# A long convolution beside an MLP on one core: the two octet transforms as one block, on three fixed two-bank PSUM tiles that the MLP's first product shares

## The chip, the cores and the metric

The kernel runs on one core of a Trainium2 chip. The metric is device microseconds (us) of one launch. Before the change the median of three runs is 364.56 us (364.38 to 364.85).

A core has a matrix engine (TensorE; PE in the profile, its weight loads PEld), a vector engine (VectorE; DVE), a scalar engine (ScalarE; ACT), GpSimd (POOL) and SyncE (SP). They run side by side and wait for each other through semaphores. Matrix products land in PSUM, which this kernel allocates in eight banks of 512 float32 numbers per partition; everything else is computed from SBUF. SP, ACT and POOL each issue transfers between DRAM and SBUF. Each engine works through its own list of instructions in order: an instruction that waits holds up all that stand behind it on that engine.

## The reference, cut to what matters

```
# S = 2048 rows, D = 448 channels, F = 1792, all float32
xn  = layernorm(q)
ks  = shift conv of k with 4 taps           # per channel
kv  = ks * v
y   = causal convolution of kv with ssm_k (length 2048, by FFT of 4096) + ssm_D * kv
out = q + xn * y + (mish(xn @ w1 + b1) @ w2)
```

There are two branches, a gated long convolution and a two-layer MLP, and their sum with q is the output.

## The kernel before, in words

**The MLP** sets the beat. The rows are taken in 8 chunks of 256, and F in 7 pieces of 256, which makes 56 pairs (chunk, piece), and two *slots* for each pair. Each float32 operand of a product is split in a high and a low part, and three products are added. In the even slot 2i stands `g1_mm(i)` (L499): 22 matmuls of 256 columns into one PSUM bank, the hidden layer transposed. In the odd slot 2i+1 stand `mish(i)` and `g2_mm(i-2)`. `mish` is, on ACT, two activations (L507) that read that bank and a cast to the high part `ach` (L79), and on DVE the low part `acl` (L80). `g2_mm` is 12 matmuls of 448 columns (L528 to L530) into two further banks, where the output of a chunk is summed.

For the first five chunks the normalised rows are transposed on PE: `ln_T` (L452) writes four small transposes into a bank of the same pool as `g1_mm`'s, ACT casts it to `XH` (L464), and DVE subtracts to `XL` (L462). That happens twice for a chunk, each time for 128 of its rows: T0 behind the `g1_mm` of the last pair but one of the chunk ahead, T1 just before the `g1_mm` of its last pair. Chunk 0 is transposed at the start in other banks.

**The convolution** is an FFT written as float32 matmuls in small tiles, put into the slots by hand: `at(slot, ...)` puts a piece ahead of the MLP's instructions of that slot, `after(slot, ...)` behind them. It has three stages.

- *F1* (slots up to 59): blocks of 8 small matmuls (L130; the profile shows each small float32 matmul as two, x16) on the filter `h` and on `kv`; ACT copies one half (L136), DVE folds (L140), and the results go to DRAM as `Dh` and `Dkv`.
- *The octets* (slots 63 to 90): eight parts. For octet o a block H transforms the filter (`ah`, read from `Dh`) and a block V the signal (`av`, read from `Dkv`). Both are `f2_mm` (L219), 16 small matmuls of 448 columns each (x32 in the profile), in two halves, real and imaginary. ACT copies both results to SBUF as `hs` (L230) and `vs` (L239). DVE multiplies them (`prod`, L252 for its arithmetic). A block I1 (L262), of 16 more, goes back; ACT copies its result to `qe` (L270) and issues two stores of it to `E` in DRAM (L273). V stands at slot s = 65, 68, ..., 86, H one slot earlier (63 for the first), I1 at s + 4. The last I1 stands at slot 90.
- *I2* (slots 98, 102, 106, 110): POOL loads `e` from `E` (L295), DVE folds (L301, L303), a block of 8 small matmuls for each of two chunks (L319) finishes the convolution, and DVE gates it and adds it to the rest.

**PSUM before:** `g1p`, two tiles of one bank, for `g1_mm`, the transposes and the fillers at the start; `g2p`, two of one bank; `pcp`, two tiles `pc` of two banks, that all of F1, F2, I1 and I2 take in turn. A tile is handed out anew for each use, and a use waits until the tile's last reader is done.

**At the start** `g1_mm(0)` writes both banks of `g1p`, its two column blocks in turn, and each of the first two activations reads one of them; ACT casts weights (L354) between these two.

## Time and profile before

| what | value |
|---|---|
| median of three runs | 364.56 us (364.38 to 364.85) |
| the profiled execution, its own time | 364.74 us |
| its span, from first to last instruction | 363.0 us |
| mean granted TensorE clock | 0.999 |
| busy: DVE, ACT, POOL | 74%, 46%, 20% of the span |
| g1 matmuls (XH by w1h, one of the groups) | 448 of 285 ns, 90.6 us |
| F2 matmuls on ah; on av | 256 of 542 ns; 256 of 543 ns |
| stores of E, from issue to landing | 5.8 us each |

The span is the time from the first to the last instruction; 1.7 us of the execution's time lie around it. In a row of the timeline the first number is the start, the second the length; matmuls overlap, so that a row's length is more than its share of the engine. `[0.62 <-ACT XH L464]` at a row's end says that the engine stood idle for 0.62 us before it and what ended that. `<-` in a row puts the output before the inputs. A view of windows gives, for each stretch, its length, then PE, PEld, DVE, ACT and POOL busy with instruction counts, then the granted clock, the DMA share and GB/s. In a row of the groups stand, after the count, the busy time and the mean ns of one, then the idle time before and its releaser.

### The profile page before, as it was taken

How to read it: one execution, taken by the hardware profiler on the slowest of the kernel's cores; microseconds unless marked ns; L12 is line 12 of the kernel's file. 1: busy time of each engine (PE TensorE's matmuls, PEld its weight loads, DVE VectorE, ACT ScalarE, POOL GpSimd, SP SyncE). 2: the span in 40 equal slices, each digit the busy share in tenths (PEclk: the TensorE clock that was granted, in tenths of full speed). 3: DMA queues.
4: the chain of work that ended last, by engine and by line, in shares of the span. 5: the costliest groups of instructions: out<-in, count | busy, mean ns of one | idle time of the engine just before them, and what ended most of it. 6: DMA issues, size and time to landing. Idle time of an engine off the chain costs nothing.

```text
span 363.0 us, 7466 instructions
## 1 busy us (share of the span) xinstructions
PE 357.0 (98%) x3108; PEld 290.0 (80%) x3108; DVE 268.0 (74%) x367; ACT 166.6 (46%) x279; POOL 71.4 (20%) x66
## 2 busy tenths in 40 slices
PE   8999999999999999999999999999999999999995
PEld 2988888888888988988977666666666889889885
DVE  5999658999998988797427755767665744997641
ACT  4966553343424323334254555647655534225450
POOL 2136003722037224513000020000010005112020
PEclk9999999999999999999999999999999999999999
DMA  7998969758686438615877798998897486969655
GB/s 247 363 369 307 414 248 275 182 175 270 156 260 199 105 101 255 152 60 144 226 245 231 252 257 210 289 258 218 284 283 172 93 251 216 404 246 279 105 71 132
DMA packets 32451, 81.69 MB, mean 225 GB/s; under 512 B 2977, under 2 KB 18978, under 8 KB 32418
## 3 DMA queue, kind: packets, MB, share of 16 engines
q1 hardware_dynamic: 21266, 47.16, 39.3%
q10 hardware_dynamic: 8240, 19.38, 21.8%
q0 software_dynamic: 2912, 14.69, 13.5%
q8 instruction: 24, 0.39, 0.5%
q14 instruction: 9, 0.07, 0.1%
HBM read 52.77 MB, written 28.45 MB: 224 GB/s over the span
## 4 chain that ended last, share of the span: by engine, by line
PE 49%; DMA 4%; DVE 2%; ACT 1%; ACTq 1%; issue 0%
PE pg L499 18%; PE pg L528 7%; PE pc L219 6%; PE pg L530 6%; PE pg L529 6%; PE pc L262 4%; PE pc L319 2%; DMA av<-Dkv 2%; DMA Dkv<-st 2%; ACTq L273 1%; DVE st L140 1%; DVE x L183 1%; ACT a L507 0%; DVE qt L535 0%; DVE x L186 0%
## 5 line engine op out<-in xcount | busy, mean ns | idle before, releaser
L507 ACT ACTIVATE a<-pg,b1t 128x256 f32<-128x256 f32 x112 | 47.2, 473 | 108.7 <-PE pg L499 95.4
L499 PE MATMUL pg<-XH,w1h 128*128 128x256 f32 x448 | 90.6, 285 | 0.2 <-DVE XL L462 0.2
L499 PEld LDWEIGHTS pg<-XH,w1h 128*128 128x128 f32 x448 | 69.6, 188 | 18.6 <-issue 16.5
L528 PE MATMUL pg<-w2h,ach 128*128 128x448 f32 x224 | 83.2, 371 | 0.0
L530 PE MATMUL pg<-w2h,acl 128*128 128x448 f32 x224 | 81.4, 363 | 0.0
L80 DVE TENSOR_TENSOR acl<-a,ach 128x512 fp32r<-128x512 f32 x56 | 39.1, 698 | 57.1 <-ACT ach L79 57.0
L529 PE MATMUL pg<-w2l,ach 128*128 128x448 f32 x224 | 81.2, 362 | 0.0
L499 PE MATMUL pg<-XL,w1h 128*128 128x256 f32 x448 | 71.3, 277 | 0.0
L499 PEld LDWEIGHTS pg<-XL,w1h 128*128 128x128 f32 x448 | 60.2, 188 | 0.0
L499 PE MATMUL pg<-XH,w1l 128*128 128x256 f32 x336 | 56.8, 278 | 0.0
L528 PEld LDWEIGHTS pg<-w2h,ach 128*128 128x128 f32 x224 | 42.0, 187 | 14.4 <-issue 11.5
L499 PEld LDWEIGHTS pg<-XH,w1l 128*128 128x128 f32 x336 | 46.8, 188 | 0.0
L530 PEld LDWEIGHTS pg<-w2h,acl 128*128 128x128 f32 x224 | 42.1, 188 | 2.6
L529 PEld LDWEIGHTS pg<-w2l,ach 128*128 128x128 f32 x224 | 42.1, 188 | 2.4
L140 DVE TENSOR_TENSOR st<-pc,st 128x896 f32<-128x896 f32 x32 | 34.8, 1089 | 4.5 <-ACT st L136 3.8
L79 ACT CAST ach<-a 128x512 fp32r<-128x512 f32 x56 | 34.7, 620 | 1.8
L166 POOL TENSOR_TENSOR x<-kr,skb 128x896 f32<-128x896 f32 x8 | 17.0, 2130 | 78.2 <-DVE x L165 56.8
L183 DVE TENSOR_TENSOR x<-x 128x896 f32<-128x896 f32 x24 | 26.4, 1098 | 2.8 <-POOL x L166 2.2
L403 POOL TENSOR_TENSOR mv<-ve,mhalf 128x2 f32<-128x2 f32 x3 | 3.8, 1251 | 98.1 <-DVE ve L400 98.1
L136 ACT COPY st<-pc 128x896 f32<-128x896 f32 x16 | 14.5, 907 | 14.2 <-PE pc L130 12.6
L407 POOL TENSOR_SCALAR xn<-qt,mv,rstd 128x448 f32<-128x448 f32 x8 | 20.5, 2566 | 0.4
L270 ACT COPY qe<-pc 128x896 f32<-128x896 f32 x16 | 13.8, 912 | 12.0 <-PE pc L262 12.0
(83 smaller groups left out, 384.4 us busy)
## 6 DMA issues: line engine op xcount, KB each, us to landing
Dkv<-st ACTq DMA_DIRECT2D x16, 448.0 KB, 6.3
ah<-Dh SPq DMA_DIRECT2D x8, 896.0 KB, 7.9
av<-Dkv SPq DMA_DIRECT2D x8, 896.0 KB, 6.9
E<-qe ACTq DMA_DIRECT2D x16, 448.0 KB, 5.8
e<-E POOLq DMA_DIRECT2D x8, 896.0 KB, 8.4
kr<-in_k_dram SPq DMA_DIRECT2D x10, 448.0 KB, 6.4
Dh<-st ACTq DMA_DIRECT2D x10, 448.0 KB, 5.9
x<-in_hT_dram SPq DMA_DIRECT2D x8, 448.0 KB, 6.5
```

Of the source, the lines that this page charges most:

```text
L79: nc.scalar.copy(h, raw)
L80: V.tensor_sub(l, raw, h)
L140: f(st[:, n], e, st[:, 1])
L166: nc.gpsimd.tensor_mul(o, KR[g - u // 2], skb[:, u:u + 1].to_broadcast([128, 2, D]))
L183: V.tensor_add(KV[g], KV[g], o)
L219: nc.tensor.matmul(p[32 * t:32 * t + 32, r, :D], g[rs, t, c], a[rs, t], start=True, stop=True, tile_position=(64 * r, 32 * t))
L407: eng.tensor_scalar(xn[:, jj, :D], Q[c][:, jj], mv[:, j, 0:1], rs(c)[:, jj:jj + 1], op0=ALU.subtract, op1=ALU.mult)
L499: nc.tensor.matmul(ps[n], l, r, start=all(m[0] != n for m in seq[:n_]), stop=all(m[0] != n for m in seq[n_ + 1:]))
L507: nc.scalar.activation(a[:, n], ps[n], AF.Mish, bias=b1t[:, 2 * p + n:2 * p + n + 1])
L528: nc.tensor.matmul(ps, ah[:, n, cs], w2h[:, f], start=f == 0, stop=False)
L529: nc.tensor.matmul(ps, ah[:, n, cs], w2l[:, f], start=False, stop=False)
L530: nc.tensor.matmul(ps, al[:, n, cs], w2h[:, f], start=False, stop=f == NF - 1)
```

## The change

It does five things.

1. **PSUM.** The pools `g1p` and `pcp` are gone. In their place stand three tiles of two banks that are made once, `pp`, `pq` and `pr` (`duo`). `pg()` hands out the two banks of `pp` in turn to `g1_mm`, the transposes and the fillers. F1 takes `pq` and `pr`, I2 too.
2. **The octets.** H and V of an octet are one block `hv_mm` at slot s = 66, 69, ..., 87: H in two tiles, then V in two, of which one is a tile that H has just used, behind its copy by ACT. For even s the order of the tiles is pp, pq, pr, pp; for odd s pr, pq, pp, pr. I1 of octet o-1 stands at s + 2, and the last at slot 90: I1 of octet 6 at slot 89. A table `GB` gives the first products in these slots banks of `pr` and `pp`.
3. **The product.** DVE reads V in PSUM, in its four multiplications; `vs` and the 16 copies to it are gone. Subtraction and addition follow. In odd slots `mish` stands ahead of the block, and its split (ACT and DVE) behind the four multiplications (`held`).
4. **The stores** of `E` are issued by POOL instead of ACT.
5. **Buffers.** `hs` has one buffer instead of two, `av`, `ya` and `yc` two instead of one. `ah` and `av` of an octet are both loaded three slots ahead (the first at 59 and 63).

```diff
-    g1p = pool("ps_g1", 2, space=PSUM)
     g2p = pool("ps_g2", 2, space=PSUM)
-    pcp = pool("ps_c", 2, space=PSUM)
+    psp = pool("ps", space=PSUM)
+    duo = [psp.tile([128, 2, 512], F32, name=n) for n in ("pp", "pq", "pr")]
...
+    def bank(n):
+        return duo[n // 2][:, n % 2]
...
+    def pg():
+        turn[0] += 1
+        return bank(turn[0] % 2)
...
-        PS[key, g] = ps = [pc(), pc()]
+        PS[key, g] = ps = [pc(1), pc(2)]
...
+    def hv_mm(o, hb, vb):
+        PS["H", o] = [f2_mm(AH[o], o, c, hb[c]) for c in range(2)]
+        h_out(o)
+        PS["V", o] = [f2_mm(AV[o], o, c, vb[c]) for c in range(2)]
+        AH.pop(o), AV.pop(o)
...
-            nc.scalar.copy(PV[o][:, c], p[:, :, :D])
...
+    def prod(o):
+        vr, vi = (p[:, :, :D] for p in PS.pop(("V", o)))
+        hs = HS.pop(o)
...
+        for x, *y in ((a, vr, hr), (c, vr, hi), (b, vi, hi), (e, vi, hr)):
+            V.tensor_mul(x, *y)
+        for fn in held:
+            fn()
...
-            nc.scalar.dma_start(E.rearrange("p (k h) d -> p k h d", h=2)[:, k:k + 4, o // 4], qe[64 * r:64 * r + 64])
+            nc.gpsimd.dma_start(E.rearrange("p (k h) d -> p k h d", h=2)[:, k:k + 4, o // 4], qe[64 * r:64 * r + 64])
...
-        pt = [g1p.tile([128, 2, CH], F32, name="pg1") for _ in range(2 if i == 0 else 1)]
+        pt = [(bank(GB[i]) if i in GB else pg()).rearrange("p (a b) -> p a b", a=2) for _ in range(2 if i == 0 else 1)]
...
+        hb, vb, ib = ((0, 1), (2, 0), (2, 1)) if s % 2 == 0 else ((2, 1), (0, 2), (0, 2))
...
+        at(s, hv_mm, o, hb, vb)
...
+            at(s + 2, i1_mm, o - 1, ib)
...
+    at(s + 3, i1_mm, o, (0, 1))
+    after(s + 3, i1_out, o)
```

The order of the instructions shows what this makes of three places. A row is an instruction with its line, its output and inputs, the shape of one, how many stand in a row, and in brackets the engines (or queues) whose semaphores it waits for. Line numbers are those of each kernel's own source (g1 is L499 before and L504 after, the transposes L452 and L456, F2 L219 and L227, the `qe` copies L270 and L274). The sign `_49` belongs to the semaphores' names.

First PE at the end of chunk 0, where the second transposition T1 of chunk 1 is followed by the pair's first product. Before:

```order
L130 MATMUL pc<-x,idr 64x448 [waits DMAHW1_49,DVE_49,PE_49]
L130 MATMUL pc<-x,idr 64x448 x7
L452 MATMUL pg_544<-idr,xn 128x128 [waits Activation_49,Pool_49]
L452 MATMUL pg_544<-idr,xn 128x128 x2
L452 MATMUL pg_544<-idr,xn 128x128 [waits Pool_49]
L499 MATMUL pg_551<-XH,w1h 128x256 [waits DVE_49]
L499 MATMUL pg_551<-XH,w1h 128x256 x2
```

After:

```order
L138 MATMUL pq<-x,idr 64x448 x2
L138 MATMUL pr<-x,idr 64x448 x2
L456 MATMUL pp<-idr,xn 128x128 [waits DVE_49,Activation_49,Pool_49]
L456 MATMUL pp<-idr,xn 128x128 x2
L456 MATMUL pp<-idr,xn 128x128 [waits Pool_49]
L504 MATMUL pp<-XH,w1h 128x256 [waits DVE_49]
L504 MATMUL pp<-XH,w1h 128x256 x2
```

The rows keep their places; the tile is now one, `pp`, for both. Before, the DVE semaphore's value at L499 was that of the subtraction `XL` of T0, whose bank the product takes over; in the program after, it is that of `XL` of T1, which reads the transposes that stand just ahead. So it is at each of the four chunk changes with transposes. Elsewhere `g1_mm(i+1)` waits in the program after for the second activation of `mish(i)`, where it waited for that of `mish(i-1)`, or of none, before; and at the start the first activation waits for all of `g1_mm(0)`, where it waited for its own bank's part.

Then PE in the octets. Before, a V block behind the odd slot's `g2_mm` (H stands in the same form one slot earlier):

```order
L528 MATMUL pg_2085<-w2h,ach 128x448
L529 MATMUL pg_2085<-w2l,ach 128x448
L530 MATMUL pg_2085<-w2h,acl 128x448
L219 MATMUL pc<-av,g 32x448 [waits DMAHW1_49,Activation_49]
L219 MATMUL pc<-av,g 32x448 x7
L219 MATMUL pc<-av,g 32x448 [waits Activation_49]
L219 MATMUL pc<-av,g 32x448 x7
L499 MATMUL pg_2344<-XH,w1h 128x256 x3
```

After, the block of an odd slot:

```order
L227 MATMUL pr<-ah,g 32x448 [waits DMAHW2_49,DMAHW1_49]
L227 MATMUL pr<-ah,g 32x448 x7
L227 MATMUL pq<-ah,g 32x448 [waits Activation_49]
L227 MATMUL pq<-ah,g 32x448 x7
L227 MATMUL pp<-av,g 32x448 [waits DMAHW3_49,Activation_49]
L227 MATMUL pp<-av,g 32x448 x7
L227 MATMUL pr<-av,g 32x448 [waits Activation_49]
L227 MATMUL pr<-av,g 32x448 x7
L536 MATMUL pg_2008<-w2h,ach 128x448
```

H and V stand in one piece, and V's last half waits for ACT, which copies H out of the same tile.

Last ACT at the end of the octets, the copies and stores of octets 6 and 7. Before:

```order
L270 COPY qe<-pc 128x896 [waits DMAHW7_49,DMAHW6_49,PE_49]
L270 COPY qe<-pc 128x896 [waits PE_49]
L273 DMA E<-qe 64x4x448 [waits DMAHW0_49,Activation_49]
L273 DMA E<-qe 64x4x448 [waits DMAHW2_49]
L507 ACTIVATE a<-pg_3333,b1t 128x256 [waits PE_49]
L507 ACTIVATE a<-pg_3333,b1t 128x256
L79 CAST ach<-a 128x512 [waits Activation_49]
L270 COPY qe<-pc 128x896 [waits DMAHW2_49,DMAHW0_49,PE_49]
L270 COPY qe<-pc 128x896 [waits PE_49]
L273 DMA E<-qe 64x4x448 [waits DMAHW3_49,Activation_49]
L273 DMA E<-qe 64x4x448 [waits DMAHW4_49]
```

After:

```order
L274 COPY qe<-pp 128x896 [waits DMASW3_49,DMASW4_49,DVE_49,PE_49]
L274 COPY qe<-pr 128x896 [waits DVE_49,PE_49]
L274 COPY qe<-pp 128x896 [waits DMASW5_49,DMASW6_49,PE_49,Activation_49]
L274 COPY qe<-pq 128x896 [waits PE_49]
L512 ACTIVATE a<-pr,b1t 128x256 [waits DVE_49,PE_49]
L512 ACTIVATE a<-pr,b1t 128x256
```

The stores have left ACT's list, and the copies of octet 7 now follow directly on those of octet 6. `qe` has one buffer before and after: the copies of octet 7 wait for the two stores of octet 6 (DMASW5 and DMASW6), which used to lie three slots back and now lie one.

More of the change, by code (lines that the diff above doesn't have):

```diff
@@ L28 @@
 POOL_H = {20: (0, 2)}
-H0_AT = 63
-OCT_AT = (65, 3)
+OCT_AT = (66, 3)
 I2_AT = {98: (6, 7), 102: (0, 1), 106: (2, 3), 110: (4, 5)}
@@ L80, in split, with pc @@
         V.tensor_sub(l, raw, h)
-    def pc():
-        return pcp.tile([128, 2, 512], F32, name="pc")
+    def pc(n):
+        return duo[n]
+    def bank(n):
+        return duo[n // 2][:, n % 2]
+    turn = [0]
+    def pg():
+        turn[0] += 1
+        return bank(turn[0] % 2)
     drip = []
@@ L191, in tile_kernel @@
     sp2 = []
-    GT, AH, AV, HS, PV, Y = {}, {}, {}, {}, {}, {}
+    GT, AH, AV, HS, Y = {}, {}, {}, {}, {}
     def t2(shape, name, bufs=1):
@@ L204, in o_load @@
             GT[o] = [g]
-        d[o] = t2([128, 4, D], name)
+        d[o] = t2([128, 4, D], name, 2 if d is AV else 1)
         nc.sync.dma_start(d[o], src[16 * o:16 * o + 16].rearrange("(t a) n d -> (a n) t d", t=4))
@@ L211, in gi_load, with f2_mm @@
         GT[o].append(gi)
-    def f2_mm(a, o, c):
-        p = pc()
+    def f2_mm(a, o, c, n):
+        p = pc(n)
         g = GT[o][0]
@@ L221, in f2_mm, with h_out, i1_mm @@
         return p
-    def h2_mm(o):
-        PS["H", o] = [f2_mm(AH[o], o, c) for c in range(2)]
-        AH.pop(o)
-    def h2_out(o):
-        HS[o] = t2([128, 2, 2, D], "hs", 2)
+    def hv_mm(o, hb, vb):
[3 more added lines that the diff above has]
+        AH.pop(o), AV.pop(o)
+    def h_out(o):
+        HS[o] = t2([128, 2, 2, D], "hs")
         for c, p in enumerate(PS.pop(("H", o))):
             nc.scalar.copy(HS[o][:, c], p[:, :, :D])
-    def v2_mm(o):
-        PS["V", o] = [f2_mm(AV[o], o, c) for c in range(2)]
-        AV.pop(o)
-    def v2_out(o):
-        PV[o] = t2([128, 2, 2, D], "vs")
-        for c, p in enumerate(PS.pop(("V", o))):
-            nc.scalar.copy(PV[o][:, c], p[:, :, :D])
-    def prod(o, part):
-        vs, hs = PV[o], HS[o]
-        vr, vi, hr, hi = vs[:, 0], vs[:, 1], hs[:, 0], hs[:, 1]
-        if part == 0:
-            Y[o] = a, c, b, e = [t2([128, 2, D], n) for n in ("ya", "yc", "yb", "yd")]
-            ops = ((V.tensor_mul, a, vr, hr), (V.tensor_mul, b, vi, hi), (V.tensor_sub, a, a, b))
-        else:
-            a, c, b, e = Y[o]
-            ops = ((V.tensor_mul, c, vr, hi), (V.tensor_mul, e, vi, hr), (V.tensor_add, c, c, e))
-            del PV[o], HS[o]
-        for f, *x in ops:
-            f(*x)
-            dv()
-    def i1_mm(o):
+    def prod(o):
+        vr, vi = (p[:, :, :D] for p in PS.pop(("V", o)))
+        hs = HS.pop(o)
+        hr, hi = hs[:, 0], hs[:, 1]
+        a, c = Y[o] = [t2([128, 2, D], n, 2) for n in ("ya", "yc")]
+        b, e = [t2([128, 2, D], n) for n in ("yb", "yd")]
+        for x, *y in ((a, vr, hr), (c, vr, hi), (b, vi, hi), (e, vi, hr)):
+            V.tensor_mul(x, *y)
+        for fn in held:
+            fn()
+        held.clear()
+        dv(2)
+        V.tensor_sub(a, a, b)
+        dv()
+        V.tensor_add(c, c, e)
+        dv()
+    def i1_mm(o, ib):
         gi = GT[o][1]
-        ps = [pc(), pc()]
+        ps = [pc(n) for n in ib]
         for c in range(2):
@@ L312, in i2_mm @@
     def i2_mm(c):
-        p = pc()
+        p = pc(1 + c % 2)
         e = EE.pop(c)
@@ L469, in ln_T @@
             x_tiles(c)
-        p = g1p.tile([128, 2, CH], F32, name="pg1").rearrange("p a b -> p (a b)")
+        p = pg()
         transposes(c, jj, p)
@@ L473, in ln_T @@
             x_split(c, jj, p, lo)
-    AHL, P1, P2 = {}, {}, {}
+    AHL, P1, P2, GB = {}, {}, {}, {}
+    held, hv = [], set()
     pairs = [(c, p) for c in range(NCHUNK) for p in range(NP)]
@@ L513, in mish @@
         al = mp.tile([128, 2, CH], F32R, name="acl", bufs=3)
-        split(ah, al, a)
-        dv()
         AHL[i] = ah, al
+        if 2 * i + 1 in hv:
+            held.append(lambda: split(ah, al, a))
+        else:
+            split(ah, al, a)
+            dv()
     def g2_mm(i, jjs=(0, 1)):
@@ L564, in mlp_slot @@
                     ln_T(c + 1, 0)
-                mish(i)
+                if s not in hv:
+                    mish(i)
             if 0 <= j < n - 1:
@@ L612, in tile_kernel @@
         s, d = OCT_AT[0] + OCT_AT[1] * o, OCT_AT[1]
-        h = s - 1 if o else H0_AT
-        (at if o else after)(h - d if o else h - 4, o_load, AH, Dh, o, "ah")
-        at(s - d if o else s - 2, o_load, AV, Dkv, o, "av")
-        at(h, h2_mm, o)
-        after(h, h2_out, o)
-        at(s, v2_mm, o)
-        after(s, v2_out, o)
-        at(s, gi_load, o)
-        after(s + 1, prod, o, 0)
-        after(s + 2, prod, o, 1)
-        at(s + 4, i1_mm, o)
-        after(s + 4, i1_out, o)
+        hb, vb, ib = ((0, 1), (2, 0), (2, 1)) if s % 2 == 0 else ((2, 1), (0, 2), (0, 2))
+        (at if o else after)(s - d if o else s - 7, o_load, AH, Dh, o, "ah")
+        at(s - d if o else s - 3, o_load, AV, Dkv, o, "av")
+        at(s, hv_mm, o, hb, vb)
+        at(s, gi_load, o)
+        after(s, prod, o)
+        if s % 2:
+            hv.add(s)
+        if o:
+            at(s + 2, i1_mm, o - 1, ib)
+            after(s + 2, i1_out, o - 1)
+        if s % 2 == 0:
+            GB[s // 2], GB[s // 2 + 1] = 2, 0
+        else:
+            GB[s // 2 + 1] = 2
+    at(s + 3, i1_mm, o, (0, 1))
+    after(s + 3, i1_out, o)
+    GB[(s + 3) // 2] = 4
     ts = sorted(I2_AT)
@@ L682, in tile_kernel @@
     x_tiles(0)
-    fill = g1p.tile([128, 2, CH], F32, name="pg1").rearrange("p a b -> p (a b)")
+    fill = pg()
     def filler(n, w=wz):
@@ L714, in tile_kernel @@
             g2_evac(pairs[j][0])
+        if s in hv:
+            mish(s // 2)
         for fn, args in plan.pop(s, ()):
@@ L719, in tile_kernel @@
         for fn, args in fns:
-            if fn in (h2_out, v2_out, i1_out):
+            if fn is i1_out:
                 fn(*args)
         for fn, args in fns:
-            if fn not in (h2_out, v2_out, i1_out):
+            if fn is not i1_out:
                 fn(*args)
```

## The prediction

> **What bounds the kernel.** I read the span and the engines' shares first, then the windows (length, then PE, PEld, DVE, ACT, POOL busy, clock, DMA share, GB/s), one for the F1 stage and one for the octets.

> ```profile
> span 363.0 us, 7466 instructions
> PE 357.0 (98%) x3108; PEld 290.0 (80%) x3108; DVE 268.0 (74%) x367; ACT 166.6 (46%) x279; POOL 71.4 (20%) x66
> 20.00:160.00 140.00, 139.79 (x1087) 123.39 (x1080) 123.68 (x171) 58.83 (x104) 46.22 (x31) 1.00 0.71 224
> 185.00:290.00 105.00, 104.50 (x1143) 72.64 (x1142) 68.02 (x83) 57.87 (x87) 3.69 (x4) 1.00 0.82 234
> ```

> PE has no idle time to give: 0.21 us in 140, 0.50 in 105. So a saving counts only if PE spends less time on its own instructions, and any new wait of PE is added to the end in full, because nothing later has slack to take it back. DVE is near full only up to 160 us (123.68 of 140). The question is thus what PE now has to wait for. The order shows it: `g1_mm`, the transposes and `mish` share one tile, `pp`, and a product waits for the last reader of the whole tile, where it used to wait for the reader of its own bank.

> **Start: +2.6.**

> ```profile
> 10.95 0.48 ACT L507 ACTIVATE a<-pg,b1t 128x256 f32<-128x256 f32 x1
> 11.31 1.05 ACT L354 CAST w1h<-kr 128x1024 fp32r<-128x1024 f32 x1
> 12.25 0.48 ACT L507 ACTIVATE a<-pg,b1t 128x256 f32<-128x256 f32 x1
> 14.51 0.84 ACT L507 ACTIVATE a<-pg,b1t 128x256 f32<-128x256 f32 x2 [0.28 <-PE pg L499]
> 11.48 0.62 PE L499 MATMUL pg<-XH,w1h 128*128 128x256 f32 x3
> 14.31 0.50 PE L499 MATMUL pg<-XH,w1h 128*128 128x256 f32 x3
> ```

> The first product's second pair starts at 11.48, so pair 0 ends just ahead. Now the first activation waits for all of pair 0 (11.49 instead of 10.95, +0.54), and pair 1 for the second activation. Between them stands the cast, 12.25 − 10.95 = 1.30 from activation to activation: 11.49 + 1.30 + 0.48 = 13.27, then PE at 13.3, +1.8. Pair 1 takes 14.31 − 11.48 less its present waits, about 2.67, to 15.97; pair 2 now waits for the 0.84 of `mish(1)`: 16.9 instead of 14.31, +2.6. Before, pair 2 waited for `mish(0)` alone.

> **Four chunk changes: +10.7.** First the product behind T1, then the subtraction that ends `XL` of the same T1, for chunks 1 to 4.

> ```profile
> 38.21 0.60 PE L499 MATMUL pg<-XH,w1h 128*128 128x256 f32 x3
> 78.00 0.60 PE L499 MATMUL pg<-XH,w1h 128*128 128x256 f32 x3
> 117.97 0.60 PE L499 MATMUL pg<-XH,w1h 128*128 128x256 f32 x3
> 155.97 0.62 PE L499 MATMUL pg<-XH,w1h 128*128 128x256 f32 x3 [0.20 <-DVE XL L462]
> 39.11 0.69 DVE L462 TENSOR_TENSOR XL<-pg,XH 128x512 fp32r<-128x512 f32 x1 [0.62 <-ACT XH L464]
> 80.92 0.68 DVE L462 TENSOR_TENSOR XL<-pg,XH 128x512 fp32r<-128x512 f32 x1
> 121.37 0.68 DVE L462 TENSOR_TENSOR XL<-pg,XH 128x512 fp32r<-128x512 f32 x1
> 157.43 0.68 DVE L462 TENSOR_TENSOR XL<-pg,XH 128x512 fp32r<-128x512 f32 x1
> ```

> The product used to run while ACT cast and DVE subtracted; now it waits for both: 39.80 − 38.21 = 1.6, 81.60 − 78.00 = 3.6, 122.05 − 117.97 = 4.1, 158.11 − 155.97 = 2.1, 11.4 in all. Only the first subtraction waits for its input; the others come late because DVE has other work ahead of it. DVE doesn't stop while PE does, so at the second and fourth it may have caught up a little: I take 3.3 and 1.7, which makes 1.6 + 3.3 + 4.1 + 1.7 = 10.7. The floor, with DVE free as at the first, is 4 × 1.6 = 6.4, the ceiling 11.4. Behind the stalled product on PE stands everything else.

> **Other pairs: nothing.** The product waits for the `mish` of the pair directly ahead, which runs under `g2_mm`.

> ```profile
> 41.49 0.84 ACT L507 ACTIVATE a<-pg,b1t 128x256 f32<-128x256 f32 x2
> 43.20 0.52 PE L499 MATMUL pg<-XH,w1h 128*128 128x256 f32 x3
> ```

> The cover is 43.20 − 42.33 = 0.87 even here, behind a late `mish`. Without it a pair would cost what ACT is late.

> **One block for two: −2.9, and −0.5 of waits.** Weight loads of one block and the next product, then five pieces of the chain of waits, in order of time:

> ```profile
> 194.82 0.18 PEld L219 LDWEIGHTS pc<-ah,g 64*32 64x32 f32 x16
> 195.23 0.15 PEld L219 LDWEIGHTS pc<-ah,g 64*32 64x32 f32 x8 [0.22 <-issue]
> 195.60 0.15 PEld L219 LDWEIGHTS pc<-ah,g 64*32 64x32 f32 x8 [0.22 <-issue]
> 196.49 0.19 PEld L528 LDWEIGHTS pg<-w2h,ach 128*128 128x128 f32 x1 [0.73 <-issue]
> 302.76 2.51 PE pg L499 x22
> 307.67 2.51 PE pg L499 x22
> 312.58 1.66 PE pc L319 x32
> 319.36 2.51 PE pg L499 x22
> L219 PE MATMUL pc<-av,g 64*32 64x448 f32 x256 | 13.9, 543 | 0.5 <-DMA av<-Dkv 0.3 <-ACT hs L230 0.2
> ```

> A block of 32 small matmuls is four passes, 0.37 apart, and the product behind it starts late. Two slots without a block take 307.67 − 302.76 = 4.91, with a block 319.36 − 307.67 − 4.91 = 6.78, so that one block costs 1.87. Of that 4 × 0.375 = 1.5 are passes and 0.37 the change of tile shape. Merged, one change is saved for each octet: 8 × 0.37 = 2.9. The number of passes stays. The 0.5 of waits ahead of V goes too: both loads are now three slots ahead, and the copy it waited for no longer holds two shared tiles. Inside the block, V's last half waits for a copy of H:

> ```profile
> 207.78 1.74 PE L219 MATMUL pc<-ah,g 64*32 64x448 f32 x32
> 208.87 1.72 ACT L230 COPY hs<-pc 128x896 f32<-128x896 f32 x2 [1.87 <-PE pc L219]
> L140 DVE TENSOR_TENSOR st<-pc,st 128x896 f32<-128x896 f32 x32 | 34.8, 1089 | 4.5 <-ACT st L136 3.8
> ```

> The copies start 1.09 behind the block; the first ends at 1.09 + 0.86 = 1.95, V's last half starts six passes in, at 6 × 0.375 = 2.25. The cover is 0.3; a late ACT costs the difference. The 16 copies that go were ACT's, which has 57.87 busy of 105: nothing. DVE's multiplications now read PSUM; a DVE operation of that size with a PSUM operand takes 1.09, and DVE is idle for 37 of 105 in this stage: nothing.

> **End of the octets: +4.0.** The chain from the last I1 to I2:

> ```profile
> 290.99 1.01 PE L262 MATMUL pc<-ya,gi 32*64 32x448 f32 x16
> 292.78 1.72 ACT L270 COPY qe<-pc 128x896 f32<-128x896 f32 x2 [2.60 <-PE pc L262]
> 294.53 1.25 ACTq L273 DMA_DIRECT2D E<-qe  x2
> 302.33 2.90 POOL L295 DMA_DIRECT2D e<-E  x4 [33.33 <-DMA idr<-MR]
> 311.53 1.09 DVE L303 TENSOR_TENSOR e<-e 128x896 f32<-128x896 f32 x1
> E<-qe ACTq DMA_DIRECT2D x16, 448.0 KB, 5.8
> Dh<-st POOLq DMA_DIRECT2D x6, 448.0 KB, 8.6
> ```

> I2 (312.58 in the chain) starts before the last fold ends at 312.62, and its second chunk half a block, 0.83, later: the slack is some 0.7. In the change I1 of octet 7 starts at the same slot; call that U. I1 of octet 6 starts one slot, 2.4 for `g2_mm` and 1.87 for the block, sooner, at U − 4.3, and its copies end, as before, 294.50 − 290.99 = 3.5 later, at U − 0.8. The copies of octet 7 wait until both its stores have landed, the second issued 0.6 behind. For a store I take 6.7, between the 5.8 that ACT's took in this stage and POOL's 8.6 for one of this size, and nearer to the first for the sake of the stage: landed at U − 0.8 + 0.6 + 6.7 = U + 6.5, copied by U + 8.2, where the copies ended at U + 3.5. The last two stores then take 7.3, about what they take now (302.33 − 294.53, less 0.6 to the load's issue, is 7.2). So 4.7 late, less the slack, 4.0. With 5.8 for a store the copies are 3.8 late, the last stores 0.8 sooner: 2.3. With 8.6 they are 6.6 late, the last stores 2.0 later: 7.9. The first half of that wait holds ACT's queue, so `mish(45)` and the products behind it; they are the same loss, not another.

> **Sum.** +2.6 + 10.7 − 2.9 − 0.5 + 4.0 = +13.9; the profiled execution took 364.74, which makes 378.6. It lies 0.18 above the median of the runs, so against that the forecast is **378.5**. Low ends: 2.6 + 6.4 − 3.4 + 2.3 = +7.9, 372.5. High ends, without the waits of V saved: 2.6 + 11.4 − 2.9 + 7.9 = +19.0, 383.6. Without these extremes at once, the likeliest case alone spans 375 to 382.

> **Rivals.**

> *The waits don't bite (faster).* If a product at a chunk change effectively waits only for its bank, the start and the chunk changes cost nothing and 364.6 − 3.4 + 2.3 to 4.0 remain: 363.5 to 365.2. For it: the text hands out single banks in turn, as before. Against: the built order has the semaphore's value of the late subtraction. It is faster only where the end costs under 2.7. Chance 6%.

> *The clock falls in a gap.* The third gap, 4.1 us, is the longest that PE has had since its start. [...]

> ```profile
> L660 PE MATMUL pg<-wz 128*8 128x448 f32 x6 | 3.9, 819 | 1.0 <-DVE wz L656 1.0
> ```

> Four passes of the F2 block with 448 columns start 0.37 apart (above), these take 0.82 each. If PE then ran at that rate for as long as those six take, 3.9 us, it would lose about half of that, 1.9: 380.4. [...] The trace of before has no such gap to show it. Chance 12%.

> *POOL's stores are slow.* With 8.6 for a store the end costs 7.9 instead of 4.0: 382.4. For it: POOL issued those at 8.6 while DMA was busy, as here (0.82). Against: ACT's own took 5.8 in this very stage. [...] Chance 15%.

> *ACT is late for V's last half*, so the block is not one piece: `mish` stands ahead in odd slots, 0.84 and 0.6 of cast, and takes the cover of 0.3. If it costs 0.6 for each octet, 8 × 0.6 = 4.8: 383.3, and the change doesn't do what it says. Chance 10%.

> **Chances.** The sum as it stands 57%, the four rivals 43% together. A measurement of this kernel tells a difference from none at about 0.2%, 0.7 us; only the first rival can end there or below. Faster 0.05, same 0.02, slower 0.93. The range, 373.5 to 384, leaves out most of the first rival and the extremes of the terms.

> **What would show it.** Start: pair 2's first product near 16.9. Chunk changes: four idle stretches of PE that end with DVE's `XL`, together near 10.7, the third the longest. Blocks: 64 F2 records in one piece in some 3.4 us, and no wait for ACT in it. End: copies of octet 7 that wait for a store, and an idle stretch ahead of the first I2 of about 4. A granted clock under 0.99 would speak for the second rival; gaps missing at the chunk changes would overthrow the forecast.

## The result: 8% slower, and where the 30 us went

The changed kernel takes 394.48 us (392.75 to 395.26, six runs) against 364.71 us for the kernel before in the same runs: a ratio of 1.081, 95% interval 1.0783 to 1.0836. The forecast was 378.5 us, its range 373.5 to 384.0. The sign was right, the size was short by half.

First the span, the busy shares and the granted clock in 40 slices, from the page of the changed kernel:

```profile
span 393.0 us, 7444 instructions
PE 367.0 (93%) x3108; PEld 300.4 (76%) x3108; DVE 266.5 (68%) x367; ACT 153.2 (39%) x263; POOL 81.0 (21%) x82
PEclk9899899996999969997999999999999999999999
```

PE executes the same 3108 matmuls as before and yet is busy for 10 us more (367.0 against 357.0): some of them ran slowly. The rest of the 30 us between the spans is idle time. What PE waits for, with total, times and longest, from the view of waits of the changed kernel (L504 is g1, L456 the transposes, L466 `XL`, L512 the activations, L274 the copies to `qe`); the last row is ACT's:

```profile
PE pp L504 <- DVE XL L466: 13.3, 4, 4.6
PE pp L504 <- ACT a L512: 3.3, 3, 1.9
PE pp L456 <- ACT a L512: 2.0, 2, 1.5
PE pp L504 <- ACT qe L274: 1.4, 1, 1.4
ACT a L512 <- DVE XL L466: 6.4, 4, 2.4
```

The first row is the forecast's main term, four waits for `XL`. The third and the last were not in it. The pairs' start times in the two timelines show where the lateness arises. Each row is the start, in us, of a pair's first product (pairs counted from 0); "late" is after less before:

| pair | before | after | late | added since the row above |
|---|---|---|---|---|
| 1 | 11.48 | 13.43 | 1.95 | 1.9 |
| 2 | 14.31 | 18.71 | 4.41 | 2.5 |
| 5 | 31.32 | 35.86 | 4.54 | 0.1 |
| 6 (change 1) | 38.21 | 44.76 | 6.55 | 2.0 |
| 7 | 43.20 | 51.38 | 8.18 | 1.6 |
| 12 | 71.08 | 79.25 | 8.18 | 0.0 |
| 13 (change 2) | 78.00 | 91.54 | 13.53 | 5.4 |
| 14 | 83.09 | 98.73 | 15.64 | 2.1 |
| 20 (change 3) | 117.97 | 138.58 | 20.61 | 5.0 |
| 21 | 122.96 | 146.10 | 23.14 | 2.5 |
| 27 (change 4) | 155.97 | 182.95 | 26.98 | 3.8 |
| 28 | 162.21 | 191.56 | 29.35 | 2.4 |
| 31 | 178.18 | 207.62 | 29.44 | 0.1 |
| 45 (last I1) | 292.67 | 318.44 | 25.76 | −3.7 |
| 55 | 349.26 | 379.32 | 30.06 | 4.3 |

Each change adds twice: once ahead of its product, and once more while that pair runs. The octets, up to pair 45, win back 3.7, and their end loses 4.3 again, together 0.6. The second change, in PE's, DVE's and ACT's timelines of the changed kernel:

```profile
86.28 0.63 PE L456 MATMUL pp<-idr,xn 128*128 128x128 f32 x4 [0.45 <-ACT a L512]
91.54 1.01 PE L504 MATMUL pp<-XH,w1h 128*128 128x256 f32 x3 [4.62 <-DVE XL L466]
84.63 0.68 DVE L466 TENSOR_TENSOR XL<-pp,XH 128x512 fp32r<-128x512 f32 x1
86.87 0.69 DVE L79 TENSOR_TENSOR acl<-a,ach 128x512 fp32r<-128x512 f32 x1 [1.56 <-ACT ach L78]
90.80 0.68 DVE L466 TENSOR_TENSOR XL<-pp,XH 128x512 fp32r<-128x512 f32 x1
85.35 0.84 ACT L512 ACTIVATE a<-pp,b1t 128x256 f32<-128x256 f32 x2 [2.24 <-DVE XL L466]
```

This is a ring of waits through one tile. The activation reads one bank of `pp`; it waits 2.24 until DVE has read the other for the first `XL` (84.63 + 0.68). The cast behind it is late, so DVE idles 1.56 ahead of `acl`; the second transposition waits for the activation (0.45); and `XL` of that transposition, for which the product waits, comes later still. Three matmuls of that product take 1.01, where the row of the kernel before had 0.60. The windows of 1 us show why (the third number from the end is the granted clock):

```profile
88.00:89.00 1.00, 0.00 (x0) 0.00 (x0) 0.97 (x3) 0.34 (x1) 0.00 (x0) 1.00 1.08 391
90.00:91.00 1.00, 0.00 (x0) 0.00 (x0) 1.00 (x2) 0.00 (x0) 0.00 (x0) 0.50 1.01 125
94.00:95.00 1.00, 1.00 (x7) 1.00 (x6) 0.00 (x0) 0.00 (x0) 0.00 (x0) 0.50 0.00 0
97.00:98.00 1.00, 1.00 (x7) 0.94 (x6) 0.00 (x0) 0.97 (x2) 0.00 (x0) 1.00 0.00 0
```

The clock falls to 0.50 while PE idles and stays there until 96.2, although PE works without a gap from 91.54. So it goes in this execution behind every one of the five gaps of the first half, the start's and the four chunk changes', also behind the first chunk change's, which is 1.76 long in PE's timeline.

At the end of the octets, POOL's issues and the copies that wait, in the timelines of the changed kernel:

```profile
316.26 1.24 POOL L277 DMA_DIRECT2D E<-qe  x2 [11.41 <-ACT qe L274]
324.08 0.91 ACT L274 COPY qe<-pp 128x896 f32<-128x896 f32 x1 [8.12 <-DMA E<-qe]
326.09 1.24 POOL L277 DMA_DIRECT2D E<-qe  x2 [8.59 <-ACT qe L274]
333.11 2.88 POOL L299 DMA_DIRECT2D e<-E  x4 [5.78 <-DMA E<-qe]
```

The page's part on transfers has their median:

```profile
E<-qe POOLq DMA_DIRECT2D x16, 448.0 KB, 5.8
```

As forecast, the copies of octet 7 wait for the stores of octet 6, here for 8.12 us. The median hides that the two stores of a pair differ: the second of octet 6 was issued at 316.9, and the copies could start only at 324.08, some 7.2 later. And the merged block, in PE's timeline, with the product behind it:

```profile
304.17 0.98 PE L227 MATMUL pr<-ah,g 64*32 64x448 f32 x16
306.45 0.96 PE L227 MATMUL pr<-av,g 64*32 64x448 f32 x16
307.34 0.47 PE L536 MATMUL pg<-w2h,ach 128*128 128x448 f32 x1
```

Its 64 records take 307.34 − 304.17 = 3.17 us in one piece and wait for nothing. One block of the kernel before cost 1.87, of which 0.21 lay ahead of and behind its 1.66; 3.17 + 0.21 = 3.38 against 2 × 1.87 = 3.74 is 0.36 saved, as forecast. The other seven merged blocks take 3.17 to 3.20 as well.

### The profile page after: what moved, and what is told of

Same layout as the page of the kernel before. It is cut to its first block, busy times and chain, and to the rows that moved or that the text cites. A ratio compares the mean times of both kernels' runs of the same rounds, so it can differ in the third digit from the quotient of the medians.

```text
span 393.0 us, 7444 instructions
## 1 busy us (share of the span) xinstructions
PE 367.0 (93%) x3108; PEld 300.4 (76%) x3108; DVE 266.5 (68%) x367; ACT 153.2 (39%) x263; POOL 81.0 (21%) x82
## 4 chain that ended last, share of the span: by engine, by line
PE 45%; DMA 5%; DVE 3%; issue 1%; ACT 1%; POOL 0%; POOLq 0%; ACTq 0%
PE pp L504 12%; PE pg L536 6%; PE pg L538 5%; PE pq L504 5%; PE pg L537 5%; DMA E<-qe 3%; PE pp L227 2%; PE pr L227 2%; PE pp L266 2%; PE pq L227 2%; DMA e<-E 1%; PE pr L266 1%; PE pr L323 1%; PE pq L323 1%; DVE ex L305 1%
## 5 line engine op out<-in xcount | busy, mean ns | idle before, releaser
L504 PE MATMUL pp<-XH,w1h 128*128 128x256 f32 x376 | 80.3, 298 | 18.1 <-DVE XL L466 13.3
L512 ACT ACTIVATE a<-pp,b1t 128x256 f32<-128x256 f32 x94 | 39.5, 471 | 123.8 <-PE pp L504 105.4
L504 PEld LDWEIGHTS pp<-XH,w1h 128*128 128x128 f32 x376 | 62.5, 200 | 32.2 <-DVE XL L466 14.3
L504 PE MATMUL pp<-XL,w1h 128*128 128x256 f32 x376 | 64.0, 290 | 0.0
L504 PEld LDWEIGHTS pp<-XL,w1h 128*128 128x128 f32 x376 | 54.7, 201 | 0.0
L504 PE MATMUL pp<-XH,w1l 128*128 128x256 f32 x282 | 50.6, 290 | 0.0
L504 PEld LDWEIGHTS pp<-XH,w1l 128*128 128x128 f32 x282 | 42.3, 202 | 0.0
L148 DVE TENSOR_TENSOR st<-pq,st 128x896 f32<-128x896 f32 x32 | 34.8, 1089 | 3.7 <-ACT st L144 2.8
L78 ACT CAST ach<-a 128x512 fp32r<-128x512 f32 x56 | 34.8, 621 | 1.7
L277 POOL DMA_DIRECT2D E<-qe x16 | 10.0, 628 | 74.9 <-ACT qe L274 74.9
L144 ACT COPY st<-pr 128x896 f32<-128x896 f32 x16 | 14.5, 908 | 13.7 <-PE pr L138 12.6
L512 ACT ACTIVATE a<-pq,b1t 128x256 f32<-128x256 f32 x16 | 6.7, 471 | 31.9 <-PE pq L504 31.9
## 6 DMA issues: line engine op xcount, KB each, us to landing
Dkv<-st ACTq DMA_DIRECT2D x16, 448.0 KB, 4.7
E<-qe POOLq DMA_DIRECT2D x16, 448.0 KB, 5.8
kr<-in_k_dram SPq DMA_DIRECT2D x10, 448.0 KB, 6.2
Dh<-st ACTq DMA_DIRECT2D x10, 448.0 KB, 5.2
x<-in_hT_dram SPq DMA_DIRECT2D x8, 448.0 KB, 6.2
```

Of the source, the lines that this page charges most:

```text
L78: nc.scalar.copy(h, raw)
L148: f(st[:, n], e, st[:, 1])
L504: nc.tensor.matmul(ps[n], l, r, start=all(m[0] != n for m in seq[:n_]), stop=all(m[0] != n for m in seq[n_ + 1:]))
L512: nc.scalar.activation(a[:, n], ps[n], AF.Mish, bias=b1t[:, 2 * p + n:2 * p + n + 1])
```

## The experiments

Nine kernels ran beside the kernel before. Times are medians, ratios those to the kernel before in the same runs.

**One bank, one tile.** The tile `pp` is made as two tiles of a bank each.

```diff
-    duo = [psp.tile([128, 2, 512], F32, name=n) for n in ("pp", "pq", "pr")]
+    class Two:
+        def __init__(self):
+            self.t = [psp.tile([128, 512], F32, name=n) for n in ("pa", "pb")]
...
+    duo = [Two()] + [psp.tile([128, 2, 512], F32, name=n) for n in ("pq", "pr")]
...
-            nc.scalar.copy(HS[o][:, c], p[:, :, :D])
+            for b, z in halves(p):
+                nc.scalar.copy(HS[o][:, c, b], z)
...
```

> The changed kernel with the tile pp made as two tiles of one bank each; all else stays, but copies and multiplications that read pp as a whole are split in two. Theory (PE waits for readers of the other bank of pp, and the clock falls to half after each such gap): the waits at the start (2.7 us) and at the four chunk changes (16.2) go, and the slow clock behind them (1.7 and 8.6) goes too, so about 394.5 - 29.2 = 365.3, granted clock 0.99 or more. Rival A (the octets or the stores from GpSimd cost the time): it stays above 385. Rival B (the clock falls for a reason that is not the gaps): the waits go, the clock stays near 0.97, about 375.

Measured: 365.57 us (364.92 to 366.36, ten runs), ratio 1.002 (1.0004 to 1.0036), granted clock 1.0. PE's busy time is back:

```profile
PE 356.5 (98%) x3108; PEld 291.1 (80%) x3108; DVE 266.6 (73%) x383; ACT 153.7 (42%) x272; POOL 80.8 (22%) x82
```

No product waits for `XL` of its own change any more, and pairs 1 to 31 start within 0.2 of the kernel before. The whole loss of 29 us hangs on the dependence between the two banks. Both rivals fall. The octets still win 3.7 here, up to pair 45, and their end still loses 3.8.

**Sharing alone.** The kernel before, in which only the two tiles of `g1p` become one.

```diff
-    g1p = pool("ps_g1", 2, space=PSUM)
+    g1t = pool("ps_g1", space=PSUM).tile([128, 2, 512], F32, name="pp")
...
+    def pg():
+        turn[0] += 1
+        return g1t[:, turn[0] % 2]
...
```

> The kernel before with one edit: the two one-bank tiles of g1p become the two banks of one tile, handed out in turn. Octets, stores and everything else as before. Theory: it takes the start and the four chunk changes of the changed kernel in full, 364.7 + 29.2 = 394, granted clock near 0.965. Rival A (sharing alone is harmless, the merge is needed): 364.7 to 368. Rival B (waits without the slow clock): 364.7 + 18.9 = 383.6.

Measured: 392.13 us (391.5 to 393.14, four runs), ratio 1.0751 (1.0728 to 1.0774), clock 0.969. The wait is the same to the tenth:

```profile
PE pp L505 <- DVE XL L468: 13.3, 4, 4.6
```

At the four changes the lateness grows by 2.00, 5.29, 4.97 and 3.83 ahead of the products and by 1.64, 2.40, 2.71 and 2.42 behind them, as in the changed kernel. At the start the gap is there too, but the clock did not fall in this execution: pair 3 is 3.40 late where it was 4.54 late in the changed kernel. That is 1.1 of the 1.6 us between the two profiled spans, 391.4 and 393.0. So the loss needs neither the merge nor the products from PSUM nor the stores.

**Filling the gaps.** Matmuls of zeros in PE's waits at the changes.

```diff
+    FILL_T0 = {13: 1, 27: 4}
+    FILL_T1 = {6: 4, 13: 12, 20: 11, 27: 6}
...
+    def keep(n):
+        for _ in range(n):
+            nc.tensor.matmul(list(P2.values())[-1][0:8, 0:224], wz, wz[:, 0:1].to_broadcast([128, 224]), start=False, stop=False)
...
+        keep(FILL_T1.get(i, 0))
...
+                        keep(FILL_T0.get(i, 0))
                         ln_T(c + 1, 1)
```

> The changed kernel with matmuls of zeros (224 columns, weights of 8 columns) put into PE's waits at the four chunk changes: 4, 12, 11 and 6 behind the second transposition, 1 and 4 ahead of it at the second and the fourth. They add zeros to the running output sum, which no other engine reads then. The waits stay as long. Theory (half clock because PE idles): the granted clock stays 1.0 at the four changes and falls only at the start; 394.5 - 8.6 = 386, or a little more where the fill outlasts a wait. Rival (the slow matmuls come from something else, such as two engines on one tile): no gain, 394 to 396, clock near 0.965.

Measured: 386.10 us (383.49 to 386.5, four runs), ratio 1.0576 (1.0538 to 1.0614), clock 1.0. The lateness added ahead of the four products is the same as in the changed kernel, 2.00, 5.33, 4.97 and 3.89; behind them it is 0.02, 0.02, 0.03 and −0.08 instead of 1.63, 2.11, 2.53 and 2.37. That is 8.65 less in all, and work that computes nothing makes the kernel 8.4 us faster by the medians. So the second loss of each change is the clock, which falls because PE idles. At the start, which was not filled, the clock did not fall in this execution either; that gain of 0.8 is lost again behind pair 31.

**Part of the gaps filled.** The same with fewer zero matmuls; the edit is against the run above.

```diff
-    FILL_T1 = {6: 4, 13: 12, 20: 11, 27: 6}
+    FILL_T1 = {6: 2, 13: 4, 20: 7, 27: 5}
```

> The changed kernel with fewer zero matmuls in the waits of the four chunk changes, so that PE idles for some 1.0, 3.4, 2.0 and 0.7 us there. Theory (the clock falls when PE has idled for more than about half of a window of 3.4 us): it falls at the second, may fall at the third, and not at the first and fourth; 388 to 390.5. Rival (any gap of about 1 us drops it): it falls at the first too, 391 or more. Rival (only a whole idle window drops it): at none, 386.

Measured: 388.53 us in a single run, clock 0.99. The clock fell at the second and the third change, each time for one window of 3.41 us, and not at the first and the fourth. PE idled for 2.88 and 1.87 us in the two windows that ended in a fall, and for 0.90 and 0.28 in those of the first and the fourth change. Both rivals fall, in this one execution; how much idleness it takes is worked out in the last section.

**Mish ahead of the first split.** In the slot of the first transposition the cast to `XH` and the subtraction to `XL` are issued behind `mish`.

```diff
+        if jj == 0:
+            return lambda: [x_split(c, jj, p, lo) for lo in range(2)]
...
-                if p == NP - 2 and c + 1 < NT:
-                    ln_T(c + 1, 0)
+                late_split = ln_T(c + 1, 0) if p == NP - 2 and c + 1 < NT else None
                 if s not in hv:
                     mish(i)
+                if late_split:
+                    late_split()
```

> The changed kernel with one order changed: in the slot of the first transposition, its cast and subtraction are issued behind mish instead of ahead of it. Theory (mish's activation, which reads the one bank of pp, waits until DVE has read the other for XL, and through the cast it delays DVE and the second transposition): the 6.4 us that ACT waits there go, the waits ahead of the second transposition (2.0) go, and the product's waits at the second and fourth change fall by some 1.5 each: about 5 less than 394.5, 389.5. Rival (the waits at the changes hang on DVE's own queue alone, as the prediction had it): 393.5 or more.

Measured: 384.55 us (384.32 to 386.67, four runs), ratio 1.0559 (1.0532 to 1.0587), 9.9 less than the changed kernel where 5 were expected. ACT waits for `XL` no more, and PE less:

```profile
PE pp L506 <- DVE XL L466: 9.2, 4, 3.2
PE pp L456 <- DVE XL L466: 1.3, 1, 1.3
```

Ahead of the four products the lateness added is 0.36, 1.78, 0.75 and 1.13 smaller, 4.0 together: the ring through ACT is real and has about the size expected. What is left ahead of them is 1.6, 3.6, 4.2 and 2.7. Behind them the lateness added is 1.62, 0.57, 1.01 and 2.45 smaller: with shorter gaps the clock falls at two changes instead of four. That part was not expected. The profiled execution is the slowest of the four, 386.67: at the start its clock stayed down for two windows, and pair 5 is 6.03 late instead of 4.54.

**Octet 7 in a free buffer.** One-bank tiles as above, and:

```diff
-        qe = t2([128, 4, D], "qe")
+        qe = t2([128, 4, D], "ah" if o == NO - 1 else "qe")
```

> Pp as two one-bank tiles, and the copy of octet 7's I1 goes to the buffer of ah, which is free by then, instead of waiting for the stores of octet 6 from qe. Theory (the end of the octets costs 4.0 through that wait, the merge saves 3.4): 4.0 less than with one-bank tiles alone, 361.3, faster than before by 3.4. Rival (the late end hangs on GpSimd's stores or on the place of the last two I1, not on the buffer): as with one-bank tiles alone, 365 or more.

Measured: 361.87 us (361.28 to 362.22, four runs), ratio 0.9924 (0.9907 to 0.9942): 3.7 less than one-bank tiles alone, and faster than the kernel before. From pair 31 to pair 45, over the eight octets, this kernel gains 0.36 + 3.24 = 3.6 on the kernel before. Then it loses 0.7 at the first I2, whose weights wait for the folds of chunk 7:

```profile
309.67 0.11 PEld L340 LDWEIGHTS pr<-ex,i 64*32 64x32 f32 x2 [0.22 <-DVE ex L322]
310.76 0.11 PEld L340 LDWEIGHTS pr<-e,i 64*32 64x32 f32 x2 [0.60 <-DVE e L324]
```

**The stores back on ACT.** As the last, but `E` is stored by ACT.

```diff
-            nc.gpsimd.dma_start(E.rearrange("p (k h) d -> p k h d", h=2)[:, k:k + 4, o // 4], qe[64 * r:64 * r + 64])
+            nc.scalar.dma_start(E.rearrange("p (k h) d -> p k h d", h=2)[:, k:k + 4, o // 4], qe[64 * r:64 * r + 64])
```

> One-bank tiles and octet 7's copy in the buffer of ah (361.87), and the stores of E issued by ACT as in the kernel before. Theory (the last pair of stores takes 9.1 us from GpSimd here, 291.62 to 300.75, against 7.8 from ACT before, and I2 waits 0.8 for them): 361.0. Rival (the issuing engine makes no difference): 361.6 to 362.1.

Measured: 364.26 us (361.98 to 365.64, twelve runs), ratio 0.9982 (0.996 to 1.0003). Both expectations missed; the stores on ACT cost 2.4 by the medians, with a wide spread. The place in the profiled execution (364.68), in ACT's timeline:

```profile
274.15 3.05 ACTq L294 DMA_DIRECT2D E<-qe  x2
277.31 0.84 ACT L529 ACTIVATE a<-pa,b1t 128x256 f32<-128x256 f32 x2 [3.19 <-PE pq L241]
```

and in the view of PE's waits:

```profile
PE pa L241 <- ACT a L529: 1.5, 1, 1.5
```

Two issues took 3.05, not the usual 1.25, and held ACT; the activation behind them starts at 277.31 instead of 275.19 in the kernel above, and V's half block in the tile that it reads waits 1.5. A second loss, 0.8, stands at the first I2: with the octets late, the last stores are issued 1.4 later than in the kernel above. The median store is no slower (5.2 against 5.7). What held the issue is not shown, nor how often it happens in the other eleven runs. The kernel before has one such pair too, in ACT's and PE's timelines:

```profile
219.99 2.98 ACTq L273 DMA_DIRECT2D E<-qe  x2
225.36 1.42 PE L219 MATMUL pc<-av,g 64*32 64x448 f32 x24 [0.20 <-ACT hs L230]
```

There it cost PE 0.2, ahead of a V block, against 1.5 here, which suggests that the merged block has less cover for a late ACT.

**Half of the blocks apart.** As with octet 7 in the free buffer, but in odd slots V stands behind the second product.

```diff
+        AH.pop(o)
+        if hb[0] == 0:
+            v_mm(o, vb)
+
+    def v_mm(o, vb):
         PS["V", o] = [f2_mm(AV[o], o, c, vb[c]) for c in range(2)]
-        AH.pop(o), AV.pop(o)
+        AV.pop(o)
...
+        if s % 2:
+            after(s, v_mm, o, vb)
```

> As with one-bank tiles and octet 7's copy in the buffer of ah (361.87), but in the four octets of odd slots V stands behind the slot's second product instead of directly behind H. Theory (a change of tile shape costs 0.37, and the merge saves one for each octet): 4 x 0.37 = 1.5 more, 363.4. Rival (the merge as such saves nothing; the gain over the kernel before is the shorter waits and fewer copies): 361.5 to 362.2.

Measured: 369.45 us (369.1 to 371.81, six runs), ratio 1.0141 (1.0117 to 1.0166): 7.6 more, far over the 1.5, so that both expectations missed. The run does not isolate the change of shape. V comes later by the slot's second product, the multiplication too, and the next I1 waits for it, as PE's weight loads show:

```profile
236.00 0.15 PEld L287 LDWEIGHTS pr<-ya,gi 32*64 32x64 f32 x4 [0.83 <-DVE yd L270]
```

Two octets, one of them apart, cost 1.3 to 2.0 more, and the last I1 another 2.5. The merge is worth more than its shape in this arrangement, since I1 waits as soon as V comes later. The 0.36 saved by a merged block stands on the block lengths in the timelines, not on this run; that it is the price of the change of tile shape is not shown.

**Loads of q later.** As with octet 7 in the free buffer, with two loads of q five slots later.

```diff
-        at(ts[0] - (6 if c < 2 else 4), q_load, c, nc.sync if c < 2 else nc.gpsimd)
+        at(ts[0] - (1 if c < 2 else 4), q_load, c, nc.sync if c < 2 else nc.gpsimd)
```

> As with one-bank tiles and octet 7's copy in the buffer of ah (361.87), and the loads of q for the first two chunks, which start at 289.7 and 290.1 beside the last stores of E, are moved from slot 92 to slot 97. Theory (these loads slow the last stores, which land 7.4 and 8.0 us after their issue against a median of 5.7, and I2 waits 0.8 for the folds behind them): the stores land 1.5 sooner and I2 waits no more, 361.1. Rival (the stores are slow for another reason, or the loads then slow the loads of e instead): 361.6 or more.

Measured: 361.92 us (360.87 to 363.51, six runs), ratio 0.9931 (0.9906 to 0.9955): no gain. The last stores do land sooner, 5.6 after their issue instead of 8.0, and POOL issues the loads of `e` earlier:

```profile
298.21 2.88 POOL L316 DMA_DIRECT2D e<-E  x4 [5.46 <-DMA idr<-MR]
```

That was 300.75 with the loads of q early. But the first of these loads of `e` then lands at 305.5, against 305.7: what one transfer gained the next one lost. That fits the rival's second branch, loads of `e` slowed by the loads of q beside them.

## Why the prediction failed, step by step

Two steps failed. The sum had no term for the clock, which took 10.3 us, and it put the chunk changes at 10.7 where they took 16.2. Term by term:

- **The start, +2.6: right.** Pair 2 is 4.4 late. Some 1.7 of that is the clock, half of one window of 3.41, and the other 2.7 are waits; where the clock stayed up at a start like this (sharing alone, gaps filled, part filled) they are 2.8 to 3.0.
- **Four chunk changes, +10.7: right mechanism, mis-sized.** The lateness ahead of the four products is 2.0 + 5.4 + 5.0 + 3.8 = 16.2, over the stated ceiling of 11.4, and the second is the longest, not the third. The term put DVE's old times against PE's old times, and so took for granted that DVE keeps its times. It doesn't: the activation waits for DVE's first `XL`, and with it `acl` and the second transposition. The changed program has that wait, between two readers of one tile on different engines, and the prediction did not follow it. With `mish` issued first, 4.0 of the 5.5 too little go, and the 1.6, 3.6, 4.2 and 2.7 that are left are nearly the old times of `XL` (1.6, 3.6, 4.1 and 2.1). The 0.7 that DVE was to catch up did not come.
- **Other pairs, nothing: right.** Between the changes the lateness grows by 0.0.
- **One block for two, −2.9 and −0.5: right.** The octets gain 3.7 in the changed kernel, and 3.6 to 3.7 with one-bank tiles. Of the waits ahead of V, 0.2 came from the slow pair of ACT's stores shown above, not only from the shared tiles.
- **End of the octets, +4.0: right, with some luck.** It cost 4.3; freeing octet 7 from the wait gives 3.7 and leaves 0.7 at I2. The store that held the copies took some 7.2 instead of 6.7, and they ended at 325.8, 9.1 behind I1's start at 316.75, where 8.2 were forecast. The last stores then took 6.4 to the load's issue, where 7.3 were: the two errors cancel. Octets and end together add 0.6 to the lateness; the terms made 4.0 − 3.4 = 0.6.
- **The clock, a rival at 12% with 1.9 us: the step that failed most.** It was given one gap, the longest, and one half-rate stretch of about 4 us. The half rate itself was right (0.50 granted), though it was read from a mean length, 0.82, set against a distance between starts, 0.37, and at the kernel's first matmuls, for which the windows of before show no clock below 1.00. The sign that the prediction named for it came, a granted clock under 0.99: it was 0.965. It fell in five gaps, of 1.8 us and more, and stayed down for one or two windows of 3.4: 1.7 at the start and 1.6 + 2.1 + 2.5 + 2.4 = 8.6 at the changes, 10.3 in all. The filled gaps show that the 8.6 are the clock's.

The forecast plus what these two steps lacked, 378.5 + 5.5 + 10.3 = 394.3, is the 394.5 measured. That sum is read from one trace and tests nothing; the tests are the one-bank tiles, sharing alone and the filled gaps.

The new order of the octets, then, was a gain of 3.6 all along. It was buried under a dependence that came with how the tiles were cut: with one-bank tiles and a free buffer for the last octet the same idea runs in 361.87 us.

## What to carry to other kernels

When two uses that alternate are put into one tile, look up for each reader and writer of that tile whom it waits for now, two readers included, and follow that wait once around all the engines before adding up old times. A stall of PE can have a second price, 1.6 to 2.5 us at each of the four changes here, because the clock falls: either keep stalls short (from full clock no window with 1.71 us of idleness or less ended in a fall here), or fill them. A saving on the engine that is the bound can be real and not show; test it alone before it is dropped.

## What the runs showed of the hardware

```profile
41.59:45.00 3.41, 1.65 (x22) 0.70 (x14) 2.39 (x3) 2.37 (x4) 0.00 (x0) 1.00 1.01 418
45.00:48.41 3.41, 3.41 (x18) 3.41 (x18) 2.18 (x2) 0.51 (x1) 0.00 (x0) 0.50 1.02 418
89.37:92.78 3.41, 1.24 (x6) 1.25 (x7) 3.34 (x5) 0.00 (x0) 0.00 (x0) 0.50 0.98 256
92.78:96.20 3.42, 3.42 (x18) 3.42 (x18) 0.82 (x1) 0.00 (x0) 0.00 (x0) 0.50 0.21 83
```

In the 14 windows that ended in a fall (changed kernel, sharing alone, mish first, partial fill; those at a kernel's end left out) PE idled for 1.76 to 3.41 us of the 3.41. Windows of 0.8 to 1.71 us idle, from full clock, did not end in one, nor did two of 1.78 and 1.81. So in these runs the bound lies at about 1.8 of the 3.41, and a gap's cost depends on how the windows happen to cut it. The start's gaps dropped the clock in two of five profiled executions, where 1.94 and 1.88 us of idleness fell into one window; in the other three it was 1.55 to 1.81. With mish first, the stall of 2.7 us at the fourth change was cut into 1.31 and 1.40, and the clock stayed up. The changed kernel's six runs fit this: three with a mean clock of 0.965 take 394.80 to 395.26, three with 0.969 or 0.970 take 392.75 to 394.15.

**In these runs it rose behind windows with at most 0.2 us of idleness.** From half clock, windows with 0.0 to 0.2 us idle ended in a rise, and windows with 0.93 to 2.2 us idle did not (in the changed kernel 0.0 five times against 2.17, 1.42 and 1.42). That is why the second, third and fourth changes pay for two windows each: the end of the gap reaches into the next window, as in the third row above, and keeps the clock at half there.

**Some issues of stores took 3 us of ACT.** In each of the three profiled executions in which ACT issues the stores of `E` (before, sharing alone, stores on ACT) one pair of issues of the eight took 2.98 to 3.05 us; the usual pair takes 1.25. None of GpSimd's pairs did so in the other eight executions (1.24 to 1.27 in the changed kernel). With merged blocks the long pair delayed PE by 1.5, with separate ones by 0.2 in the kernel before.
